# Regrouping the weight loads of a one-core decode step: larger rows, 128 partitions for wo, earlier issue

## The chip, the cores and the metric

One core of a Trainium2 chip runs the whole kernel. The metric is the device time of one execution in microseconds. The profiler's span of the same execution is about 2 us shorter (577.9 against 579.73 in the profiled run of the kernel before). Each run carries a state: slow when it lies more than 1.5% above the fastest run of the same kernel, else fast. The times come from several chips of the same kind, so kernels are compared where possible on one chip, together with runs of the kernel before.

In the views, PE is the matrix engine (TensorE) and PEld its weight loads, DVE is VectorE, ACT is ScalarE, POOL is GpSimd, and SP is the engine that issues the loads (SPq: its waits). A packet is one row that one DMA engine moves (the 256 K and V tiles of 128 rows are 32768 packets of 6144 bytes). The chain of waits is the work that ended last, followed backwards, at each step to what released it; its shares are shares of the span. The granted clock is PE's clock in the profile as a share of full speed (mean 0.976 in the profiled run of the kernel before). Partitions are the rows of a tile in on-chip memory: the K and V tiles have 128, wo_b has 64.

## The reference

A decode step for 4 sequences with a hidden size of 640: layer norm, then sliding-window attention over a K/V cache (32 heads of 192, a window of 2048 positions) and a SwiGLU feed-forward block in parallel, both added to the input.

```python
xn = layernorm(x)                                # [4, 1, 640], bf16 inputs
q = (xn @ wq).reshape(B, Sq, 32, 192)            # wq [640, 6144]
k = k_cache[:, :, Sk - 2048:, :]                 # [4, 32, 2048, 192], v the same
p = softmax(q @ k.T * 192 ** -0.5)
attn = (p @ v).reshape(B, Sq, 6144) @ wo         # wo [6144, 640]
ffn = (silu(xn @ w1) * (xn @ w3)) @ w2           # F = 1536
return x + attn + ffn
```

K and V are 201 of the 223 MB that are read. The weights are the other 22 MB.

## The kernel before

The work is cut into 128 units (32 heads by 4 sequences). Per unit DVE multiplies the K tile with the broadcast q, PE sums the products over the head dimension with identity matmuls (the "adder"), DVE reduces, ACT takes exponentials, and PE multiplies with the V tile (o_ps, here "p@v"). Eight units (two heads) make a group. There are 16 groups, and each needs 384 columns of wq and 384 rows of wo. The program is written in slots. A scheduler turns it into one fixed instruction order per engine at compile time. All loads are issued by one engine (SP) into one queue, in order; 16 DMA engines work on it. The code is shortened; a comment that starts with "..." says what was left out.

```python
def load_k(u):                                   # V alike: 128 partitions, rows of 6144 bytes
    kt = kpool.tile([P, NJ, Dh], BF16, tag="kt")
    nc.sync.dma_start(out=kt[:], in_=k_win[b, h].rearrange("(p j) d -> p j d", p=P))

def wq_load(hg):                                 # rows of 768 bytes
    wt = wpool.tile([P, KC, QW], BF16, tag="w")
    nc.sync.dma_start(out=wt[:], in_=A_wq[:, hg * QW:(hg + 1) * QW].rearrange("(kc p) n -> p kc n", p=P))

def wo_load(hg):                                 # rows of 1280 bytes; DA = 128, Dh - DA = 64
    wo_rows = A_wo[hg * QW:(hg + 1) * QW, :].rearrange("(h d) n -> d h n", d=Dh)
    wo_a = wopool.tile([DA, HG, D], BF16, tag="wo_a")
    nc.sync.dma_start(out=wo_a[:], in_=wo_rows[0:DA])
    wo_b = wopool.tile([DB, HG, D], BF16, tag="wo_b")       # 64 partitions
    nc.sync.dma_start(out=wo_b[:], in_=wo_rows[DA:Dh])

def ge_tot(hg):                                  # per group: row sums of the softmax, on PE
    tb = ps_t.tile([P, G], FP32, tag="t")
    nc.tensor.matmul(tb[:], lhsT=ones_ff[:], rhs=rsums.pop(hg)[:], start=True, stop=True)
    o_raw = ...                                  # ... cut: copy of o_ps, then ge_tr transposes it (gp),
                                                 # ge_copy normalises it, ge_proj multiplies with wo (acc)
# ... cut: the w1 and w3 chunks are loaded inside the slot that uses them (rows of 1024 bytes),
# ... cut: w2 is loaded in three parts behind everything else (rows of 1280 bytes)
```

## Time and profile before

| | before |
|---|---|
| time, median of 4 runs | 580.06 us (579.49 to 581.16) |
| mean load rate over the span | 386 GB/s |
| PE, DVE, ACT busy | 84%, 57%, 18% |
| share of DMA in the chain of waits | 74% |

The first fence has lines of the profile page of the kernel before: busy time by engine, the load rate in 40 equal slices of the span, the load queue (packets, MB, share), and the chain of waits by engine.

```profile
PE 488.1 (84%) x2391; PEld 204.7 (35%) x2391; DVE 330.1 (57%) x385; ACT 106.7 (18%) x407; POOL 3.5 (1%) x18
...
GB/s 308 416 406 417 405 378 407 395 371 403 369 408 409 376 412 370 417 402 384 406 376 416 373 409 407 370 410 365 418 385 394 407 374 414 367 418 400 390 370 136
...
q1 hardware_dynamic: 59552, 222.98, 100.2%
...
DMA 74%; PE 15%; DVE 8%; ACT 1%; SPq 1%; issue 1%; DVEq 0%; ACTq 0%
```

The queue is busy for the whole span (100.2% of 16 engines) and the chain of work that ended last is mostly loads. The kernel is bound by its loads. The slices show that the rate is not even: between the second slice and the last but one it swings between 365 and 418 GB/s.

The windows view of the same run shows where. Its columns are the stretch in us, then its length, the busy time and count for PE, weight loads, DVE, ACT and POOL, then the granted clock, the DMA share and GB/s.

```profile
60.00:65.00 5.00, 3.34 (x16) 1.40 (x17) 3.15 (x5) 0.18 (x1) 0.00 (x0) 1.00 1.02 417
190.00:195.00 5.00, 5.00 (x27) 2.01 (x26) 3.01 (x4) 0.96 (x2) 0.00 (x0) 1.00 1.04 302
225.00:230.00 5.00, 4.99 (x26) 2.06 (x25) 3.09 (x5) 0.96 (x2) 0.00 (x0) 1.00 1.05 304
```

From 60 to 65 us only K and V tiles are loaded: 417 GB/s. At 190 and at 225 us a wo load passes: 302 and 304 GB/s, although the DMA engines are as "busy" as elsewhere (1.04 and 1.05). Busy DMA engines are not fast DMA engines.

### The profile page before, as it was taken

The numbers are of one execution on the slowest core, as the hardware profiler recorded it, in microseconds if no ns is written. First come the engines' busy times: TensorE is split into PE (matmuls) and PEld (weight loads), VectorE is DVE, ScalarE is ACT, GpSimd is POOL, SyncE is SP. The second block draws the span as 40 slices with busy tenths as digits, with TensorE's granted clock in tenths as the row PEclk, the third lists the DMA queues.
The fourth block names the chain that finished last, engine by engine and source line by source line (L and its number), as shares of the span: only waits on it lengthen the run. The fifth ranks groups of instructions, "written<-read, shape, count | busy, mean of one in ns | idle before, by whom it ended". The sixth has DMA issues, their size and how long they took to land.

```text
span 577.9 us, 6288 instructions
## 1 busy us (share of the span) xinstructions
PE 488.1 (84%) x2391; PEld 204.7 (35%) x2391; DVE 330.1 (57%) x385; ACT 106.7 (18%) x407; POOL 3.5 (1%) x18
## 2 busy tenths in 40 slices
PE   2989889799798889797798988889897888978796
PEld 0334333233334334333343433334333333433343
DVE  4976645536555565565646565565555656656511
ACT  4122121312242202121021211102121120211110
POOL 2000000000000000000000000000000000000000
PEclk9999998969999999999998989999899999999999
DMA  8999999999999999999999999999999999999993
GB/s 308 416 406 417 405 378 407 395 371 403 369 408 409 376 412 370 417 402 384 406 376 416 373 409 407 370 410 365 418 385 394 407 374 414 367 418 400 390 370 136
DMA packets 59581, 223.37 MB, mean 386 GB/s; under 512 B 5016, under 2 KB 26784, under 8 KB 59552
## 3 DMA queue, kind: packets, MB, share of 16 engines
q1 hardware_dynamic: 59552, 222.98, 100.2%
q8 instruction: 18, 0.29, 0.2%
q14 instruction: 11, 0.09, 0.0%
HBM read 222.96 MB, written 0.01 MB: 386 GB/s over the span
## 4 chain that ended last, share of the span: by engine, by line
DMA 74%; PE 15%; DVE 8%; ACT 1%; SPq 1%; issue 1%; DVEq 0%; ACTq 0%
DMA kt<-in_A_k_cache_dram 52%; DMA vt<-in_A_v_cache_dram 12%; DVE pr L193 6%; PE ps L207 6%; DMA wt<-in_A_wq_dram 5%; PE o_ps L264 4%; DMA w3t<-in_B_w_dram 2%; DMA wo_b<-in_A_wo_dram 2%; DVE sc L216 1%; PE qp L177 1%; SPq L105 1%; PE bp L186 1%; PE acc L311 1%; PE f L419 0%; PE ut L340 0%
## 5 line engine op out<-in xcount | busy, mean ns | idle before, releaser
L193 DVE TENSOR_TENSOR pr<-kt,qbc 128x3072 bf16<-128x3072 bf16 x128 | 224.5, 1756 | 146.4 <-DMA kt<-in_A_k_cache_dram 142.9
L264 PE MATMUL o_ps<-vt,z 128*16 128x384 bf16 x1024 | 203.2, 330 | 45.9 <-DMA vt<-in_A_v_cache_dram 41.9
L207 PE MATMUL ps<-pr,idb 128*128 128x512 bf16 x768 | 199.2, 393 | 23.4 <-DVE sc L216 22.3
L207 PEld LDWEIGHTS <-idb 128*128 128x128 bf16 x768 | 70.4, 99 | 160.9 <-issue 106.4
L264 PEld LDWEIGHTS <-z 128*16 128x16 bf16 x1024 | 82.5, 90 | 119.8 <-issue 59.9
L216 DVE TENSOR_REDUCE sc<-ps 128x16 f32<-128x512 f32 x128 | 87.2, 682 | 0.9 <-PE ps L207 0.9
L242 ACT ACTIVATE negm<-mt 128x4 f32<-128x4 f32 x32 | 5.5, 173 | 254.9 <-PE mt L239 254.9
L187 ACT CAST qbc<-bp 128x384 bf16<-128x384 f32 x64 | 28.9, 478 | 50.2 <-PE bp L186 50.2
L250 ACT ACTIVATE z<-sc,negm 128x16 bf16<-128x16 f32 x128 | 37.8, 297 | 1.1
L272 ACT COPY o_raw<-o_ps 16x384 f32<-16x384 f32 x16 | 7.5, 467 | 106.2 <-PE o_ps L264 106.2
L233 DVE TENSOR_REDUCE gmax<-mt 4x1 f32<-4x128 f32 x32 | 8.8, 275 | 31.2 <-PE mt L228 31.2
L250 ACT ACTIVATION_READ_ACCUMULATOR z<-sc,negm 128x1 f32 x128 | 23.9, 187 | 0.0
L295 DVE TENSOR_TENSOR oT<-gp,rtb 128x8 bf16<-128x8 f32 x16 | 2.7, 167 | 30.9 <-PE gp L288 30.9
L186 PE MATMUL bp<-qsb,idb 4*128 4x384 bf16 x64 | 19.3, 341 | 1.1 <-ACT qsb L179 0.9
L177 PE MATMUL qp<-wt,xnT 128*4 128x384 bf16 x80 | 17.2, 349 | 0.3 <-DVE xnT L166 0.3
L278 DVE RECIPROCAL rtb<-tb 128x8 f32<-128x8 f32 x16 | 3.3, 207 | 24.4 <-PE tb L270 24.4
L239 PEld LDWEIGHTS mt<-idf,gmax 4*128 4x128 f32 x64 | 9.3, 182 | 10.1 <-issue 8.9
L239 PE MATMUL mt<-idf,gmax 4*128 4x4 f32 x64 | 12.1, 258 | 0.4 <-DVE gmax L233 0.4
L311 PE MATMUL acc<-wo_a,oT 128*4 128x512 bf16 x32 | 12.4, 388 | 0.0
L311 PE MATMUL acc<-wo_b,oT 64*4 64x512 bf16 x32 | 12.2, 381 | 0.0
L186 PEld LDWEIGHTS <-idb 4*128 4x128 bf16 x64 | 5.0, 93 | 17.9 <-issue 13.7
L311 PEld LDWEIGHTS <-oT 128*4 128x4 bf16 x64 | 5.1, 80 | 13.7 <-issue 11.8
(67 smaller groups left out, 151.3 us busy)
## 6 DMA issues: line engine op xcount, KB each, us to landing
kt<-in_A_k_cache_dram SPq DMA_DIRECT2D x128, 768.0 KB, 14.1
vt<-in_A_v_cache_dram SPq DMA_DIRECT2D x128, 768.0 KB, 14.0
wt<-in_A_wq_dram SPq DMA_DIRECT2D x16, 480.0 KB, 14.6
wo_a<-in_A_wo_dram SPq DMA_DIRECT2D x16, 320.0 KB, 14.2
wo_b<-in_A_wo_dram SPq DMA_DIRECT2D x16, 160.0 KB, 13.7
w1t<-in_B_w_dram SPq DMA_DIRECT2D x3, 640.0 KB, 13.9
w3t<-in_B_w_dram SPq DMA_DIRECT2D x3, 640.0 KB, 14.7
w2t<-in_B_w_dram SPq DMA_DIRECT2D x3, 640.0 KB, 11.9
```

What stands on the lines that cost most here:

```text
L177: nc.tensor.matmul(qp[:], lhsT=xnT[:, kc, :], rhs=wt[:, kc, :], start=(kc == 0), stop=(kc == KC - 1))
L186: nc.tensor.matmul(bp[:], lhsT=idb[0:B, b:b + 1].to_broadcast([B, P]), rhs=qsbs[hg][:], start=True, stop=True)
L187: nc.scalar.copy(out=qbcs[hg][:, b, :], in_=bp[:])
L193: mi = nc.vector.tensor_tensor(out=pr[:], in0=kts.pop(u)[:], in1=qbcs[hg][:, b, hl * Dh:(hl + 1) * Dh].unsqueeze(1).to_broadcast([P, NJ, Dh]),
L207: nc.tensor.matmul(ps[:, e], lhsT=idb[:], rhs=pr[:, :, kk * DD:(kk + 1) * DD], start=(kk == 0), stop=(kk == NK - 1))
L216: ri = nc.vector.tensor_reduce(out=scs[t][:, off:off + UPT, :], in_=pss.pop(m)[:], axis=AX.X, op=ALU.add)
L233: nc.vector.tensor_reduce(out=gmax[:], in_=chs[t][1][0:SB, 0:P], axis=AX.X, op=ALU.max)
L239: nc.tensor.matmul(mt[:, P:P + SB], lhsT=gmax[:, 0:1].to_broadcast([SB, P]), rhs=idf[0:SB, 0:SB], start=True, stop=True)
L250: nc.scalar.activation(out=zs[u % NZ][:, :, 2 * (G - 1):2 * G], in_=sc[:, b, :].rearrange("p (jj two) -> p jj two", two=2), func=ACTF.Exp, ...
L264: nc.tensor.matmul(o_ps[:], lhsT=z[:, jj, 2 * (G - 1 - g):2 * (2 * G - 1 - g)], rhs=vt[:, 2 * jj:2 * jj + 2, :], start=(g == 0 and jj == 0 ...
L272: nc.scalar.copy(out=o_raw[:], in_=o_pss.pop(hg)[:])
L311: nc.tensor.matmul(acc0[:], lhsT=lt, rhs=wo_t[:, hl, 0:N0], start=st, stop=sp)
```

## The change

The intent: fewer and larger packets for all weights, and weights there before they are needed. The diff is shortened, and its lines in plain words sum up what stands there.

```diff
-    def wq_load(hg):
-        wt = wpool.tile([P, KC, QW], BF16, tag="w")
+    def wq_load(ci):                       # first group alone, then 4 groups per load: rows of 3072 bytes
+        wt = wpool.tile([P, KC, cn * QW], BF16, tag="w")
...
     def wo_load(hg):
-        wo_a = wopool.tile([DA, HG, D], BF16, tag="wo_a")
-        nc.sync.dma_start(out=wo_a[:], in_=wo_rows[0:DA])
-        wo_b = wopool.tile([DB, HG, D], BF16, tag="wo_b")
-        nc.sync.dma_start(out=wo_b[:], in_=wo_rows[DA:Dh])
+        wo_t = wopool.tile([NPW, RW * D], BF16, tag="wo")          # NPW = 128, RW = 3: rows of 3840 bytes
+        nc.sync.dma_start(out=wo_t[:], in_=A_wo[hg * QW:(hg + 1) * QW, :].rearrange("(p r) n -> p (r n)", r=RW))
...
     def ge_tr(hg):                         # o_raw now bf16; output rows dealt out so that wo's rows are contiguous
-        4 fp32 matmuls into gp
+        for i in range(RW):
+            for h in range(HG):            # 12 small bf16 matmuls
+                nc.tensor.matmul(gp[h * PH:(h + 1) * PH, i, :], lhsT=o_raw[:, i:Dh:RW], ...)
     def ge_proj(hg, hl):
-        8 matmuls with wo_a and wo_b per group
+        6 matmuls with wo_t per group
...
-            add(uf - G - 2, 0, wq_load, hg)
+            if wq_chunks[ci][0] == hg:
+                add(max(uf - 2 * G, -KPF), 0, wq_load, ci)         # issued earlier
+    add(fs - 4, 0, ffn_load, "w1")         # w1 and w3 whole: rows of 3072 bytes, ahead of their use
+    add(fs - 2, 0, ffn_load, "w3")
...
-    w2 in three loads, rows of 1280 bytes
+    w2t = wpool.tile([P, FC, D], BF16, tag="w")                    # one load, rows of 15360 bytes
+    nc.sync.dma_start(out=w2t[:], in_=B_w2.rearrange("(p c) n -> p c n", c=FC))
```

More of the change, by code (lines that the diff above doesn't have):

```diff
@@ L41 @@
     RLAG: int = 2,
+    WBUFS: int = 3,
+    WQG: int = 4,
 ):
@@ L70 @@
     N1 = D - N0
+    DH2 = Dh // 2
+    assert Dh % 2 == 0 and DH2 <= P
     KPF = KBUFS - 1
@@ L74 @@
     const = ctx.enter_context(tc.tile_pool(name="const", bufs=1))
-    wpool = ctx.enter_context(tc.tile_pool(name="wstream", bufs=3))
+    wpool = ctx.enter_context(tc.tile_pool(name="wstream", bufs=WBUFS))
     kpool = ctx.enter_context(tc.tile_pool(name="kt", bufs=KBUFS))
@@ L106, in load_v @@
         vts[u] = vt
-    def wq_load(hg):
-        wt = wpool.tile([P, KC, QW], BF16, tag="w")
-        nc.sync.dma_start(out=wt[:], in_=A_wq[:, hg * QW:(hg + 1) * QW].rearrange("(kc p) n -> p kc n", p=P))
-        wqts[hg] = wt
-    def wo_load(hg):
-        wo_rows = A_wo[hg * QW:(hg + 1) * QW, :].rearrange("(h d) n -> d h n", d=Dh)
-        wo_a = wopool.tile([DA, HG, D], BF16, tag="wo_a")
-        nc.sync.dma_start(out=wo_a[:], in_=wo_rows[0:DA])
-        wo_b = None
-        if DB > 0:
-            wo_b = wopool.tile([DB, HG, D], BF16, tag="wo_b")
-            nc.sync.dma_start(out=wo_b[:], in_=wo_rows[DA:Dh])
-        wos[hg] = (wo_a, wo_b)
+    wq_chunks = [(0, 1)]
+    g0 = 1
+    while g0 < NG:
+        wq_chunks.append((g0, min(WQG, NG - g0)))
+        g0 += WQG
+    wq_of_group = {}
+    for ci, (cg0, cn) in enumerate(wq_chunks):
+        for gg in range(cg0, cg0 + cn):
+            wq_of_group[gg] = ci
+    def wq_load(ci):
+        cg0, cn = wq_chunks[ci]
+        wt = wpool.tile([P, KC, cn * QW], BF16, tag="w")
+        nc.sync.dma_start(out=wt[:], in_=A_wq[:, cg0 * QW:(cg0 + cn) * QW].rearrange("(kc p) n -> p kc n", p=P))
+        wqts[ci] = wt
+    RW = 3
+    PH = Dh // RW
+    NPW = HG * PH
+    def wo_load(hg):
+        wo_t = wopool.tile([NPW, RW * D], BF16, tag="wo")
+        nc.sync.dma_start(out=wo_t[:], in_=A_wo[hg * QW:(hg + 1) * QW, :].rearrange("(p r) n -> p (r n)", r=RW))
+        wos[hg] = wo_t
     x_sb = const.tile([B, D], BF16, name="x_sb")
@@ L173, in q_proj @@
     def q_proj(hg):
-        wt = wqts.pop(hg)
+        ci = wq_of_group[hg]
+        wt = wqts[ci]
+        c0 = (hg - wq_chunks[ci][0]) * QW
         qp = ps_t.tile([B, QW], FP32, tag="t")
         for kc in range(KC):
-            nc.tensor.matmul(qp[:], lhsT=xnT[:, kc, :], rhs=wt[:, kc, :], start=(kc == 0), stop=(kc == KC - 1))
+            nc.tensor.matmul(qp[:], lhsT=xnT[:, kc, :], rhs=wt[:, kc, c0:c0 + QW], start=(kc == 0), stop=(kc == KC - 1))
+        if hg == wq_chunks[ci][0] + wq_chunks[ci][1] - 1:
+            wqts.pop(ci)
         qsb = small.tile([B, QW], BF16, tag="qsb", bufs=2)
@@ L270, in ge_tot @@
         nc.tensor.matmul(tb[:], lhsT=ones_ff[:], rhs=rsums.pop(hg)[:], start=True, stop=True)
-        o_raw = small.tile([2 * G, 2 * Dh], FP32, tag="o_raw", bufs=2)
+        o_raw = small.tile([2 * G, 2 * Dh], BF16, tag="o_raw", bufs=2)
         nc.scalar.copy(out=o_raw[:], in_=o_pss.pop(hg)[:])
@@ L282, in ge_tr @@
         rtb, o_raw = ges[hg]
-        gp = ps_t.tile([P, 2 * G], FP32, tag="t")
-        nc.tensor.matmul(gp[0:DA, 0:G], lhsT=o_raw[:, 0:DA], rhs=idf[0:2 * G, 0:2 * G:2], start=True, stop=False)
-        nc.tensor.matmul(gp[0:DA, 0:G], lhsT=o_raw[:, Dh:Dh + DA], rhs=idf[0:2 * G, 1:2 * G:2], start=False, stop=True)
-        if DB > 0:
-            nc.tensor.matmul(gp[0:DB, G:2 * G], lhsT=o_raw[:, DA:Dh], rhs=idf[0:2 * G, 0:2 * G:2], start=True, stop=False)
-            nc.tensor.matmul(gp[0:DB, G:2 * G], lhsT=o_raw[:, Dh + DA:2 * Dh], rhs=idf[0:2 * G, 1:2 * G:2],
-                             start=False, stop=True)
+        gp = ps_t.tile([P, RW, G], FP32, tag="t")
+        for i in range(RW):
+            for h in range(HG):
+                nc.tensor.matmul(gp[h * PH:(h + 1) * PH, i, :], lhsT=o_raw[:, i:Dh:RW], rhs=idb[0:2 * G, 0:2 * G:2],
+                                 start=True, stop=False)
+                nc.tensor.matmul(gp[h * PH:(h + 1) * PH, i, :], lhsT=o_raw[:, Dh + i:2 * Dh:RW],
+                                 rhs=idb[0:2 * G, 1:2 * G:2], start=False, stop=True)
         ges[hg] = [rtb, gp]
@@ L293, in ge_copy @@
         rtb, gp = ges[hg]
-        oT = small.tile([P, 2 * G], BF16, tag="oT", bufs=2)
-        nc.vector.tensor_tensor(out=oT[0:DA, 0:G], in0=gp[0:DA, 0:G], in1=rtb[0:DA, :], op=ALU.mult)
-        if DB > 0:
-            nc.vector.tensor_tensor(out=oT[0:DB, G:2 * G], in0=gp[0:DB, G:2 * G], in1=rtb[0:DB, :], op=ALU.mult)
+        oT = small.tile([P, RW, B], BF16, tag="oT", bufs=2)
+        for h in range(HG):
+            ps = slice(h * PH, (h + 1) * PH)
+            cs = slice(h * B, (h + 1) * B)
+            nc.vector.tensor_tensor(out=oT[ps], in0=gp[ps, :, cs],
+                                    in1=rtb[ps, cs].unsqueeze(1).to_broadcast([PH, RW, B]), op=ALU.mult)
         ges[hg] = [oT]
@@ L301, in ge_proj @@
         oT = ges[hg][0]
-        wo_a, wo_b = wos[hg]
-        first = (hg == 0 and hl == 0)
-        last = (hg == NG - 1 and hl == HG - 1)
-        parts = [(oT[0:DA, hl * B:(hl + 1) * B], wo_a)]
-        if DB > 0:
-            parts.append((oT[0:DB, G + hl * B:G + (hl + 1) * B], wo_b))
-        for pi, (lt, wo_t) in enumerate(parts):
-            st = first and pi == 0
-            sp = last and pi == len(parts) - 1
-            nc.tensor.matmul(acc0[:], lhsT=lt, rhs=wo_t[:, hl, 0:N0], start=st, stop=sp)
+        wo_t = wos[hg]
+        n = RW // HG + (RW % HG if hl == HG - 1 else 0)
+        i0 = hl * (RW // HG)
+        for i in range(i0, i0 + n):
+            st = hg == 0 and i == 0
+            sp = hg == NG - 1 and i == RW - 1
+            lt = oT[0:NPW, i, :]
+            nc.tensor.matmul(acc0[:], lhsT=lt, rhs=wo_t[:, i * D:i * D + N0], start=st, stop=sp)
             if N1 > 0:
-                nc.tensor.matmul(acc1[:], lhsT=lt, rhs=wo_t[:, hl, N0:D], start=st, stop=sp)
+                nc.tensor.matmul(acc1[:], lhsT=lt, rhs=wo_t[:, i * D + N0:(i + 1) * D], start=st, stop=sp)
         if hl == HG - 1:
@@ L321, with ffn_load @@
     ffn_state = {}
+    def ffn_load(which):
+        wt = wpool.tile([P, KC, F], BF16, tag="w")
+        src = B_w1 if which == "w1" else B_w3
+        nc.sync.dma_start(out=wt[:], in_=src.rearrange("(kc p) n -> p kc n", p=P))
+        ffn_state[which] = wt
     def ffn_gate(nch):
-        w1t = wpool.tile([P, KC, NCH], BF16, tag="w")
-        nc.sync.dma_start(out=w1t[:], in_=B_w1[:, nch * NCH:(nch + 1) * NCH].rearrange("(kc p) n -> p kc n", p=P))
+        w1t = ffn_state["w1"]
         gt = ps_t.tile([B, NCH], FP32, tag="t")
         for kc in range(KC):
-            nc.tensor.matmul(gt[:], lhsT=xnT[:, kc, :], rhs=w1t[:, kc, :], start=(kc == 0), stop=(kc == KC - 1))
+            nc.tensor.matmul(gt[:], lhsT=xnT[:, kc, :], rhs=w1t[:, kc, nch * NCH:(nch + 1) * NCH],
+                             start=(kc == 0), stop=(kc == KC - 1))
         g_bf = small.tile([B, NCH], BF16, tag="g_bf", bufs=2)
@@ L333, in ffn_gate @@
         ffn_state[nch] = sg
+        if nch == F // NCH - 1:
+            ffn_state.pop("w1")
     def ffn_up(nch):
-        w3t = wpool.tile([P, KC, NCH], BF16, tag="w")
-        nc.sync.dma_start(out=w3t[:], in_=B_w3[:, nch * NCH:(nch + 1) * NCH].rearrange("(kc p) n -> p kc n", p=P))
+        w3t = ffn_state["w3"]
         ut = ps_t.tile([B, NCH], FP32, tag="t")
         for kc in range(KC):
-            nc.tensor.matmul(ut[:], lhsT=xnT[:, kc, :], rhs=w3t[:, kc, :], start=(kc == 0), stop=(kc == KC - 1))
+            nc.tensor.matmul(ut[:], lhsT=xnT[:, kc, :], rhs=w3t[:, kc, nch * NCH:(nch + 1) * NCH],
+                             start=(kc == 0), stop=(kc == KC - 1))
         u_bf = small.tile([B, NCH], BF16, tag="u_bf", bufs=2)
@@ L343, in ffn_up @@
         ffn_state[("u", nch)] = u_bf
+        if nch == F // NCH - 1:
+            ffn_state.pop("w3")
     def ffn_h(nch):
@@ L351, in ffn_transpose @@
         for fc in range(FC):
-            nc.tensor.transpose(out=hT_ps[:, fc, :], in_=h_sb[:, fc * P:(fc + 1) * P], identity=idb[0:B, 0:B])
+            nc.tensor.transpose(out=hT_ps[:, fc, :], in_=h_sb[:, fc:F:FC], identity=idb[0:B, 0:B])
         ffn_state["hT_ps"] = hT_ps
@@ L380 @@
         if hg >= 1:
-            add(uf - G - 2, 0, wq_load, hg)
+            ci = wq_of_group[hg]
+            if wq_chunks[ci][0] == hg:
+                add(max(uf - 2 * G, -KPF), 0, wq_load, ci)
             add(uf - G + 1, 6, q_proj, hg)
@@ L412 @@
         f1 = ps_m.tile([B, N1], FP32, tag="mt")
-    W2C = 4
-    for c0 in range(0, FC, W2C):
-        w2t = wpool.tile([P, W2C, D], BF16, tag="w")
-        nc.sync.dma_start(out=w2t[:], in_=B_w2[c0 * P:(c0 + W2C) * P, :].rearrange("(c p) n -> p c n", p=P))
-        for c in range(W2C):
-            fc = c0 + c
-            nc.tensor.matmul(f0[:], lhsT=hT[:, fc, :], rhs=w2t[:, c, 0:N0], start=(fc == 0), stop=(fc == FC - 1))
-            if N1 > 0:
-                nc.tensor.matmul(f1[:], lhsT=hT[:, fc, :], rhs=w2t[:, c, N0:D], start=(fc == 0), stop=(fc == FC - 1))
+    w2t = wpool.tile([P, FC, D], BF16, tag="w")
+    nc.sync.dma_start(out=w2t[:], in_=B_w2.rearrange("(p c) n -> p c n", c=FC))
+    for fc in range(FC):
+        nc.tensor.matmul(f0[:], lhsT=hT[:, fc, :], rhs=w2t[:, fc, 0:N0], start=(fc == 0), stop=(fc == FC - 1))
+        if N1 > 0:
+            nc.tensor.matmul(f1[:], lhsT=hT[:, fc, :], rhs=w2t[:, fc, N0:D], start=(fc == 0), stop=(fc == FC - 1))
     ffn_bf = const.tile([B, D], BF16, name="ffn_bf")
```

## The prediction

> **What bounds the kernel.** The HBM loads. The page gives one load queue with packets taking 100.2% of 16 engines' span, 223 MB at a mean of 386 GB/s; PE is busy 84%, DVE 57%; the chain of waits is 74% DMA. But 386 is an average of two regimes. In a window that holds only K and V loads (60 to 65 us, windows view) the rate is 417 GB/s; where a weight load passes it drops: 304 GB/s at 225 to 230 us and 302 at 190 to 195 us (both a wo load), about 392 near wq and w1/w3 loads. The packet records of the trace say why: a 6144-byte K/V packet takes 238 ns in clean stretches, a 768-byte packet (wq) about 39 ns, 1024 (w1, w3) 53, 1280 (wo, w2) 69: roughly 0.038 ns per byte plus 7 to 9 ns.
>
> The wo windows are worse than small packets explain: while wo_b (64 partitions) lands, K/V packets themselves stretch to 300-480 ns and wo packets from 55 to about 100. The wo_a part before it (128 partitions, the same 1280 bytes) runs at 55 ns with K/V at 238. So the main loss is the 64-partition load. [...]
>
> **What the change does to that.**
> - wo: one 128-partition load of 3840-byte rows instead of 128 + 64 partitions of 1280. From 225 to 235 us the mean is 360 GB/s against 417: 1.4 us lost per group, 16 groups, 22 us. I expect 1-2 us left: saves about 20 us.
> - wq: 768 to 3072 bytes (15 groups in 4 loads): loses about 0.3 us per group now, saves 3.5 us.
> - w1/w3: 1024 to 3072 bytes: saves 1.5 us. They also come early instead of in the slot that uses them.
> - w2: one load of 15360-byte rows: its data moves about 1 us faster, but the 24 final matmuls (12 pairs of 0.28 us) now all wait for the whole tile, so about +2 us in the tail.
> - Compute: 4 fp32 transposing matmuls per group (two passes each, 1.3 us) become 12 small bf16 ones; 8 acc matmuls become 6. Neutral within 0.5 us per group, off the critical path.
>
> As the queue is the bound, all of its saving is on the critical path until PE binds. PE's 488 us of work would be 88-89% busy. Check by packet sum: now 581 us per engine; at 239 ns per K/V packet and the line above for the larger packets, 548 (estimate). So 547 by that sum, 555 by the windows with the longer tail.
>
> **Predicted: 552 us, 8 in 10 between 543 and 563.** Faster by over 2%: 0.95; within 2%: 0.045; slower: 0.005.
>
> **What would show it.** Mean rate about 405 GB/s; no 5-us window near 300 in the middle; wo windows above 390; K/V packets averaging under 242 ns; DMA packets falling from 59.5 to about 41 thousand, with under 1000 below 2 KB apart from semaphore writes; PE about 88% busy; after the last V tile a tail of 11-13 us.
>
> **What would make it wrong.** (1) PE paces: its lumps of work fill the buffers and the queue waits for PE, so time stays near 560. (2) A 1.9 MB weight load, 4.7 us of queue, or the second wq chunk that waits for PE to free its buffer, stalls the K/V stream and the queue runs dry. (3) The wo slowdown comes from its place in the stream, not from the 64 partitions, and stays. (4) The w2 load as one tile lengthens the tail more than 2 us.

## More of the kernel before

What SP, the issuer, waits for most (the first two lines of the waits view; us in total, times, longest us):

```profile
SPq L99 <- DMA kt<-in_A_k_cache_dram: 85.4, 52, 3.0
SPq L105 <- DMA vt<-in_A_v_cache_dram: 81.4, 54, 2.5
```

It waits for older loads to land, which fits a full queue. Two of PE's waits are needed later:

```profile
PE o_ps L264 <- DMA vt<-in_A_v_cache_dram: 41.9, 51, 2.0
...
PE tb L270 <- ACT z L250: 1.6, 1, 1.6
```

PE waits 41.9 us for V tiles, and 1.6 us, once, between the exponentials and the row-sum matmul tb.

## The result

The changed kernel takes 556.0 us (median of 11 runs: three slow ones at 561.33 to 561.9, the fast ones at 552.46 to 556.2) against 580.02 us (16 runs). The ratio is 0.9571, with a 95% interval of 0.9555 to 0.9588. Such ratios are the mean time of one kernel's fast runs over that of the other's in the same rounds, so they are not quite the ratio of the medians. The lines below come from control a_again (555.93 us, ratio 0.9575).

The page of the changed kernel, the same lines as before:

```profile
PE 484.8 (87%) x2423; PEld 198.9 (36%) x2423; DVE 326.3 (59%) x385; ACT 106.6 (19%) x405; POOL 3.5 (1%) x18
...
GB/s 325 419 418 416 418 409 412 417 411 417 416 414 418 416 417 414 416 415 413 417 416 417 417 417 417 415 419 408 417 415 417 418 416 416 415 405 416 380 308 151
...
q1 hardware_dynamic: 43920, 222.98, 98.8%
...
PE 71%; DMA 12%; DVE 8%; ACT 7%; issue 1%; ACTq 0%
```

The rate is now even, 405 GB/s or more from the second slice to the thirty-seventh, and the queue's packets fell from 59552 to 43920. But the chain of waits has changed sides: 71% PE, where it was 74% DMA. In the 38th and 39th slice the rate falls to 380 and 308 GB/s, where the kernel before had 390 and 370.

Windows of the same run: K and V only, then two with a wo load.

```profile
60.00:65.00 5.00, 5.00 (x27) 2.24 (x27) 3.46 (x4) 0.17 (x1) 0.00 (x0) 1.00 1.02 420
185.00:190.00 5.00, 3.43 (x19) 1.70 (x19) 2.59 (x4) 1.44 (x9) 0.00 (x0) 1.00 1.02 418
215.00:220.00 5.00, 3.43 (x19) 1.62 (x17) 2.38 (x4) 1.45 (x9) 0.00 (x0) 1.00 1.02 415
```

The wo windows are at 418 and 415 GB/s where they were at 302 and 304. Two of PE's waits, and the first line of the issuer's:

```profile
PE tb L288 <- ACT z L268: 20.4, 13, 1.6
...
PE o_ps L282 <- DMA vt<-in_A_v_cache_dram: 4.1, 3, 2.3
```

```profile
SPq L109 <- PE o_ps L282: 75.1, 30, 5.9
```

PE hardly waits for V tiles any more (4.1 us, was 41.9), and the issuer's longest wait in total is now for PE to free a V buffer (75.1 us, was 34.2). tb's wait went from 1.6 to 20.4 us: 13 times in 16 groups PE, whose instructions stand in one compiled order, is idle for 1.6 us.

The packet records of the traces give the queue's work by packet size. This table is computed from them: packets, mean ns of one, and the sum over all packets divided by 16 engines. Its last row also has the 4-byte semaphore writes (3.0 and 2.5 us) and two small queues of instruction loads; the 125.6 ns are the mean of all 3072-byte packets together.

```
                       before                       changed (a_again)
K, V      6144 B   32768 x 246.8 = 505.5 us     32768 x 239.5 = 490.5 us
wq         768 B   10240 x  38.8 =  24.8          640 x  38.5 =   1.5
wq   3072, 2304 B                                1920 x 125.6 and 640 x 98.8 = 19.0
w1,w3     1024 B    3840 x  53.0 =  12.7         1280 x 125.6 (3072 B) = 10.1
wo, w2    1280 B    7688 x  68.8 =  33.1
wo        3840 B                                 2048 x 152.2 =  19.5
w2       15360 B                                  128 x 581.6 =   4.7
all                             580.7 us                        549.5 us
```

From the medians of the kernel before (36 ns for 768 bytes, 239 for 6144) a line has 0.038 ns per byte and 7 ns per packet, an estimate.

The queue lost 31 us of work. Half of it, 15 us, is in the K and V packets, which the change doesn't touch.

### The profile page after: what moved, and what is told of

Read it like the earlier page. It is cut to its first block, busy times and chain, and to the rows that moved or that the text cites. A ratio compares the mean times of both kernels' runs of the same rounds, so it can differ in the third digit from the quotient of the medians.

```text
span 559.6 us, 6310 instructions
## 1 busy us (share of the span) xinstructions
PE 487.7 (87%) x2423; PEld 200.1 (36%) x2423; DVE 325.4 (58%) x385; ACT 106.6 (19%) x405; POOL 3.5 (1%) x18
## 2 busy tenths in 40 slices
DMA packets 43950, 223.38 MB, mean 399 GB/s; under 512 B 4488, under 2 KB 5136, under 8 KB 43792
## 3 DMA queue, kind: packets, MB, share of 16 engines
q1 hardware_dynamic: 43920, 222.98, 98.3%
## 4 chain that ended last, share of the span: by engine, by line
PE 74%; DMA 9%; ACT 7%; DVE 7%; issue 1%; ACTq 0%
PE ps L225 31%; PE o_ps L282 29%; DVE pr L211 5%; DMA wt<-in_B_w_dram 4%; ACT z L268 3%; DMA kt<-in_A_k_cache_dram 3%; PE qp L193 3%; PE bp L204 3%; DMA vt<-in_A_v_cache_dram 3%; PE acc L329 2%; DVE sc L234 1%; ACT qbc L205 1%; ACT o_raw L290 1%; PE tb L288 1%; PE mt L257 1%
## 5 line engine op out<-in xcount | busy, mean ns | idle before, releaser
L225 PE MATMUL ps<-pr,idb 128*128 128x512 bf16 x768 | 209.1, 414 | 9.9 <-DVE sc L234 8.9
L282 PE MATMUL o_ps<-vt,z 128*16 128x384 bf16 x1024 | 210.1, 340 | 5.2 <-DMA vt<-in_A_v_cache_dram 3.3
L282 PEld LDWEIGHTS <-z 128*16 128x16 bf16 x1024 | 84.8, 92 | 132.8 <-issue 80.7
L316 DVE TENSOR_TENSOR oT<-gp,rtb 64x12 bf16<-64x12 f32 x32 | 5.4, 168 | 39.6 <-PE gp L306 39.1
L288 PE MATMUL tb<-rsum,ones_ff 128*128 128x8 f32 x32 | 6.6, 279 | 20.4 <-ACT z L268 20.4
L290 ACT CAST o_raw<-o_ps 16x384 bf16<-16x384 f32 x16 | 7.5, 467 | 80.3 <-PE o_ps L282 80.3
L193 PE MATMUL qp<-wt,xnT 128*4 128x384 bf16 x80 | 19.3, 358 | 0.7 <-DVE rtb L296 0.3
L197 ACT CAST qsb<-qp 4x384 bf16<-4x384 f32 x16 | 7.4, 464 | 61.0 <-PE qp L193 61.0
L329 PE MATMUL acc<-wo_t,oT 128*4 128x512 bf16 x48 | 16.7, 389 | 0.6 <-DVE oT L316 0.4
L304 PE MATMUL gp<-idb,o_raw 16*64 16x8 bf16 x96 | 6.3, 188 | 8.4 <-ACT o_raw L290 8.4
## 6 DMA issues: line engine op xcount, KB each, us to landing
wt<-in_B_w_dram SPq DMA_DIRECT2D x2, 1920.0 KB, 20.4
```

What stands on the lines that cost most here:

```text
L193: nc.tensor.matmul(qp[:], lhsT=xnT[:, kc, :], rhs=wt[:, kc, c0:c0 + QW], start=(kc == 0), stop=(kc == KC - 1))
L225: nc.tensor.matmul(ps[:, e], lhsT=idb[:], rhs=pr[:, :, kk * DD:(kk + 1) * DD], start=(kk == 0), stop=(kk == NK - 1))
L282: nc.tensor.matmul(o_ps[:], lhsT=z[:, jj, 2 * (G - 1 - g):2 * (2 * G - 1 - g)], rhs=vt[:, 2 * jj:2 * jj + 2, :], start=(g == 0 and jj == 0 ...
L290: nc.scalar.copy(out=o_raw[:], in_=o_pss.pop(hg)[:])
L329: nc.tensor.matmul(acc0[:], lhsT=lt, rhs=wo_t[:, i * D:i * D + N0], start=st, stop=sp)
```

## The experiments

Theory: before, the queue is the bound, and the largest loss is the 64-partition load wo_b, through what it does to the packets beside it. After, PE takes over in part, so not all of the queue's gain is seen. Rivals: small packets as such are the loss; and, for what is left, the queue is still the bound.

### a_again: the control

No edit.

> The changed kernel once more, for a profile in the fast state; a control. Expected by every theory: 552 to 557 us, DMA packets 43950, K/V packets at a mean of 240 to 241 ns. Theory 'PE took over as the bound': the chain of waits is mostly PE here too (over 50%), and the DMA rate has holes in the second half. Rival 'the queue is still the bound, only faster': the chain is mostly DMA in the fast state and the PE chain belongs to the slow state alone.

It ran in 555.93 us (4 fast runs), with K/V packets at 239.5 ns and a chain of 71% PE.

### wo_only: the kernel before with the wo part alone

```diff
# kernel before, with wo_load, ge_tot, ge_tr, ge_copy and ge_proj of the changed kernel; nothing else
```

> The kernel before with only the wo part of the change (one load of 128 partitions and 3840-byte rows, the new transposing and output matmuls). Theory 'wo_b was the main loss': about 20 of the 24 us gained, so 558 to 563 us; windows with a wo load at over 390 GB/s. Rival 'the small packets of wq, w1 and w3 matter as much': at least 568 us.

It ran in 557.09 us (557.03 to 557.17), ratio 0.9593, a little faster than the expected 558 to 563. On the same chip that is 23.3 of the 24.5 us of the whole change. Two windows, the first with all 128 packets of a wo load, the second just behind it, and the chain by engine:

```profile
185.00:190.00 5.00, 5.00 (x28) 2.19 (x27) 3.88 (x5) 0.96 (x2) 0.00 (x0) 1.00 1.01 412
190.00:195.00 5.00, 3.83 (x22) 1.69 (x19) 2.89 (x5) 1.18 (x8) 0.00 (x0) 1.00 1.02 418
```

```profile
DMA 80%; PE 10%; DVE 7%; issue 1%; ACT 1%; SPq 1%; ACTq 0%; DVEq 0%
```

With the wo load the rate is 412 GB/s, behind it 418, and this kernel is bound by the queue: its chain is 80% DMA. By the packet records the queue's work fell from 580.7 to 556.7 us, 15.2 us of it in K/V packets (246.8 to 239.4 ns). The part also takes work from PE (busy 465.5 us, was 488.1), but b_light below shows that less PE work brought the kernel before nothing.

### all_but_wo: the rest without the wo part

```diff
# changed kernel, with wo_load and the ge_ functions of the kernel before
```

> The changed kernel with the wo part put back as before (two loads, of 128 and of 64 partitions). Theory 'wo_b was the main loss': 570 to 577 us, wo windows near 300 GB/s as before. Rival 'small packets of wq, w1, w3': 562 us or less.

It ran in 575.36 us, ratio 0.9914: the rest alone is worth 5 us. A window with a wo load:

```profile
190.00:195.00 5.00, 3.43 (x19) 1.61 (x19) 2.82 (x4) 1.45 (x9) 0.00 (x0) 1.00 1.05 311
```

311 GB/s: the slow windows are back with wo_b. Alone the two parts bring 23.3 and 5.1 us, together 24.5. So 3.9 us of the sum were missing: the rest added 1.2 us to the wo part. On another chip it added more; see wo_early.

### wo1280: 128 partitions, but the old packet size

```diff
-        nc.sync.dma_start(out=wo_t[:], in_=A_wo[...].rearrange("(p r) n -> p (r n)", r=RW))
+        wo_rows = A_wo[hg * QW:(hg + 1) * QW, :].rearrange("(p r) n -> p r n", r=RW)
+        for i in range(RW):
+            nc.sync.dma_start(out=wo_t[:, i * D:(i + 1) * D], in_=wo_rows[:, i, :])
```

> The changed kernel with each wo group loaded by three loads of 128 partitions with 1280-byte rows into the same tile: the packet size of before, the partitions of after. Theory '64 partitions are what hurts': within 3 us of the changed kernel (552 to 559), 1280-byte packets at 55 to 60 ns, K/V packets beside them at 238 to 242 ns, wo windows over 395 GB/s. Rival 'the packet size of 1280 bytes hurts': wo windows near 300 GB/s and 570 us or more.

It ran in 558.45 us (553.75 to 560.16), ratio 0.9604 with an interval of 0.9552 to 0.9657. Two windows with a wo load:

```profile
185.00:190.00 5.00, 3.43 (x19) 1.62 (x18) 2.38 (x4) 1.45 (x9) 0.00 (x0) 1.00 1.03 404
215.00:220.00 5.00, 3.43 (x19) 1.59 (x18) 2.55 (x3) 1.45 (x9) 0.00 (x0) 1.00 1.03 400
```

404 and 400 GB/s, 1280-byte packets at 57.3 ns and K/V packets at 239.8 ns. In the kernel before, the same packet size gave 302 GB/s, 68.8 and 246.8 ns. The packet size is not what slowed the wo windows; it costs 2.5 us of queue work in wo's own packets (22.0 against 19.5). Nor is it wo's place in the stream or the number of its loads: the place is the same, and here there are three loads per group.

### wo64: 64 partitions, but larger packets

```diff
-    RW = 3
+    RW = 6        # 64 partitions, rows of 7680 bytes; transposes and output matmuls follow from it
```

> The changed kernel with the wo tile on 64 partitions with 7680-byte rows (one load, larger packets than in the change). Theory '64 partitions are what hurts, whatever the packet size': wo windows near 300 GB/s or lower, K/V packets beside it at 280 to 400 ns, 575 to 595 us (all of wo, not a third of it, now goes to 64 partitions). Rival 'packet size': wo windows over 395 GB/s, and within 6 us of the changed kernel, which would be PE's added small matmuls.

It ran in 617.58 us, ratio 1.0633, slower than the kernel before and slower than I expected. Two windows with a wo load:

```profile
160.00:165.00 5.00, 3.43 (x20) 1.57 (x19) 1.22 (x4) 1.45 (x9) 0.00 (x0) 1.00 1.06 223
195.00:200.00 5.00, 3.43 (x20) 1.75 (x20) 2.25 (x4) 1.45 (x9) 0.00 (x0) 1.00 1.05 221
```

223 and 221 GB/s with the largest packets that wo had in any run. One 7680-byte packet took 577 ns, as long as a 15360-byte packet of w2 on 128 partitions (586 ns in the same run): half the rate. Why 64 partitions get half, the runs do not show. The neighbours paid too: K/V packets rose to a mean of 254.2 ns; against the 239.5 of a_again that is 30 us of queue work on packets that didn't change, and wo's own packets added only 17 (19.5 to 36.9). The other weights' packets added about 6. The span grew by 61 us; the remaining 7 us are time in which the queue moved nothing, and whether the 288 added PE matmuls made it so is not tested. So the 64 partitions are the cause of the slow wo windows, and wo1280 and wo64 together rule the packet size out as the main one.

### b_light and a_light: less work for PE

```diff
-        for kk in range(NK):          # 6 adder matmuls per unit
+        for kk in range(NK // 2):     # 3: the result is wrong on purpose
```

> The kernel before with the same 3 of 6 adder matmuls left out (wrong on purpose). Theory 'the kernel before is bound by the queue': 577 to 581 us, no change. Rival 'PE was already a bound before': 573 us or less.

The kernel before took 579.08 us with half of its adder matmuls gone, ratio 0.9983 (0.994 to 1.0025). PE was no bound before.

> The changed kernel with 3 of the 6 adder matmuls per unit left out (result wrong on purpose; loads, vector work and the order of the rest as they are). Theory 'PE took over': 546 to 551 us, since the queue then is the bound; its per-engine packet sum (about 549.5 us) against 556.7 in the run with only the wo part says 7 us under that run's 557. Rival 'the queue is the bound': 554 to 557.

The changed kernel took 551.76 us with the same cut, just above the range, ratio 0.9498. This was another chip than a_again's, so the step from 555.9 is an indication and not a measurement on one chip. Its rate no longer falls at the end (416 and 422 GB/s in the 38th and 39th slice), and its chain by engine is:

```profile
DMA 58%; PE 26%; DVE 9%; ACT 5%; issue 2%; SPq 0%; ACTq 0%
```

It gives the level at which the changed loads bind: about 552 us.

### ord_tb and ord_tb_r5: tb kept behind the last p@v

```diff
# shortened: the dictionary, the helper and its guard are left out
             pv_insts[u] = nc.tensor.matmul(o_ps[:], ...)
...
-        nc.tensor.matmul(tb[:], lhsT=ones_ff[:], rhs=rsums.pop(hg)[:], start=True, stop=True)
+        ti = nc.tensor.matmul(tb[:], lhsT=ones_ff[:], rhs=rsums.pop(hg)[:], start=True, stop=True)
+        tc.add_manual_dep(ti.ins, pv_insts[hg * G + G - 1].ins.name, ORDER_DEP, reason="...")   # order only
```

> The changed kernel with one issue-order edge per group: the small matmul that sums the softmax rows (tb) may not be placed ahead of the group's last p@v matmul on PE. In the changed kernel it waits 1.6 us for the exponentials in each group, 20.4 us in all, with PE in order behind it. Theory 'PE took over, and this placing is a part of it': 549 to 552 us, that wait gone, the chain mostly DMA again, PE clock higher than 0.94. Rival 'the queue is the bound of the changed kernel and PE's waits are in its slack': 554 to 557 us as before.

It ran in 552.39 us (551.21 to 553.93), ratio 0.9516, the result correct. tb's wait is gone. The time lies just above the range of the theory (549 to 552) and below that of the rival (554 to 557), and the chain is 48% DMA and 40% PE, not mostly DMA as I had expected. For a comparison on one chip it ran again, beside the changed kernel.

> The changed kernel again, on the same chip and in the same rounds as the next three, so that they can be compared with it: 554 to 557 us by every theory.

> The changed kernel with the one issue-order edge per group, again: 551 to 553.5 us if the first measurement was no luck; its interval should now lie below that of the changed kernel. If it lies within 1 us of it, the theory that PE's order cost time in the changed kernel is left without support.

On this chip the changed kernel's four fast runs were at 551.21 to 555.42 us (mean 552.85, under the 554 to 557 that I had expected by every theory; two more, 561 and 565 us, were slow), ratio 0.9529 (0.9499 to 0.9559). ord_tb had five runs at 551.13 to 554.08 (mean 552.37), ratio 0.9521 (0.9497 to 0.9544). The difference is 0.5 us and not clear of noise: the theory that tb's place costs time gets no support from the times. The profiles do differ, but that of the changed kernel is from another chip (a_again, span 554.3 us), since the one taken on this chip was slow. Its late windows (columns as before), then those of ord_tb_r5 (span 550.4 us), then the chain by engine of ord_tb_r5:

```profile
520.00:525.00 5.00, 5.00 (x28) 2.09 (x26) 2.71 (x5) 0.00 (x0) 0.00 (x0) 1.00 0.98 360
525.00:530.00 5.00, 4.33 (x22) 1.95 (x23) 3.97 (x5) 1.45 (x9) 0.00 (x0) 1.00 0.74 246
535.00:540.00 5.00, 4.86 (x38) 2.78 (x37) 0.54 (x3) 1.45 (x9) 0.00 (x0) 1.00 0.87 289
```

```profile
525.00:530.00 5.00, 4.89 (x39) 2.66 (x37) 1.20 (x5) 0.47 (x1) 0.00 (x0) 1.00 1.01 409
535.00:540.00 5.00, 4.09 (x24) 2.03 (x23) 0.00 (x0) 0.00 (x0) 0.00 (x0) 1.00 0.93 394
```

```profile
DMA 70%; PE 21%; DVE 5%; ACT 3%; issue 1%; SPq 0%; ACTq 0%
```

In the changed kernel the queue runs dry late (360, 246 and 289 GB/s) behind a PE that is busy for 4.3 to 5.0 of 5 us; with tb behind p@v the rate stays at 409 and 394, and DMA is again 70% of the chain. The issuer's wait for PE to free V buffers is 9.6 us there, against 75.1. My reading is that the changed kernel stands where two bounds meet, near 552 us for the queue and at 552 to 556 us for PE. The times do not show it: on one chip, taking tb's waits away was worth nothing clear of noise.

### wo_early: the same wait in a kernel that the queue binds

Compiled orders compared without a run show that issuing wq early is enough to move tb ahead of p@v.

```diff
# wo_only, and
-            add(uf - G - 2, 0, wq_load, hg)
+            add(max(uf - 2 * G, -KPF), 0, wq_load, hg)
```

> The run with only the wo part, with each wq load issued 6 slots earlier and nothing else: the same packets, but in the compiled PE order the tb matmul then moves ahead of the p@v matmuls in 11 of 16 groups, as in the changed kernel (found by comparing compiled orders). Theory 'early weights moved tb, and its wait costs PE time': the wait for the exponentials at 12 to 18 us where the run with only the wo part has 1.6, and 558 to 561 us. Rival 'tb's place is harmless': 557 as before, in spite of the wait.

It ran in 557.0 us (555.6 to 557.07), ratio 0.9595, as wo_only did on another chip (0.9593). The tb wait of wo_only, then the tb wait and the chain by engine of wo_early:

```profile
PE tb L269 <- ACT z L249: 1.6, 1, 1.6
```

```profile
PE tb L269 <- ACT z L249: 17.3, 11, 1.6
```

```profile
PE 46%; DMA 41%; DVE 7%; ACT 5%; issue 1%; SPq 0%; ACTq 0%; DVEq 0%
```

The wait came as forecast, the time didn't: the rival was right. With the queue as the bound (busy for 100.0% of the span), 17 us of standing PE cost nothing. PE's busy time rose too, from 465.5 to 480.2 us for the same 2423 matmuls, at a granted clock of 0.957 in place of 0.994. And the chain went from 80% DMA to 46% PE while the time stayed: a chain that turns to PE does not by itself show that PE costs time. That holds for the changed kernel's 71% as well.

This run also gives the worth of the rest of the change on this chip: from wo_early (mean 556.7 us) to the changed kernel (552.85) it is 3.8 us, and their intervals (0.9573 to 0.9616, 0.9499 to 0.9559) do not overlap. On the first chip the rest had added only 1.2 us to wo_only.

### ord_w2: w2 and its matmuls out of the tail

```diff
# ord_tb, with the w2 load, its 24 matmuls and the two copies behind them moved from the end into the slots behind ffn_hT
```

> As the run before, and the w2 load and its 24 matmuls moved from the end to the middle of the stream. If the tail behind the last load (w2, then 24 matmuls and a copy, about 7 us) counts, 549.5 to 551.5 us: the last load is then a V tile, with some 6 us of work behind it. Rival: the moved work only displaces other work and the time stays at 552.

It ran in 553.65 us (553.28 to 553.86), ratio 0.9542 (0.9519 to 0.9565). This is a miss: if anything it is slower than ord_tb on the same chip, though the intervals overlap. The end of the chain, in order of time (start us, us, what), of ord_tb_r5 and of ord_w2:

```profile
529.92 13.55 DMA w2t<-in_B_w_dram
...
546.92 0.57 ACT ffn_bf L458
...
547.68 0.48 DVE res L469
```

```profile
534.32 9.32 DMA vt<-in_A_v_cache_dram
...
543.68 1.47 PE o_ps L287 x8
...
545.18 0.48 ACT o_raw L296
...
547.54 0.68 DVE attn_bf L468
```

In both the last load lands at 543.5 to 543.6 us. Behind w2 come 24 matmuls and two small operations, and the span ends at 550.4. Behind a V tile comes a longer chain (p@v, copy, transposes, normalising, output matmuls, casts), and it ends at 551.8. The w2 load at the end was cover for that chain.

## Why the prediction was right

- **The bound before was the queue.** Right: b_light shows it.
- **wo was the largest part, about 20 us.** Right in cause and a little small: 23.3 us in wo_only. wo1280 and wo64 show that the 64 partitions did it. The prediction had read it from K/V packets stretching beside wo_b (from 238 to 300-480 ns).
- **wq 3.5 us, w1 and w3 1.5 us, w2 about 1 us.** As work of the queue this was right: 7.2 us less between wo_only (556.7) and a_again (549.5). As time it was not all there: 1.2 us on top of the wo part on one chip, 3.8 us on another (from wo_early). So the total of the first chip was in part luck: wo brought 3 us more than said and the rest 5 us less than its 6, and the 2 us of a longer tail did not come.
- **"All of its saving is on the critical path until PE binds."** Whether the condition came true is not settled. The profile of a_again speaks for the prediction's first risk ("PE paces"): a chain of 71% PE and a rate that falls at the end. But wo_early has a chain of mostly PE at no cost, and on one chip ord_tb gained nothing clear of noise. PE was put at 88-89% busy and is at 87%. Not foreseen: the new issue order, in which PE stands for 20.4 us in tb.
- **A tail longer by 2 us.** Wrong in its mechanism. From the end of the last p@v to the end of the span it took 9.8 us before and 9.1 after. In the kernel before, the 24 matmuls with w2 stood behind the last p@v as well. By the prediction's own sign, the time after the last V tile, the packet records give 11.8 us before and 13.1 after; the growth lies ahead of the end of the last p@v, which came 2.0 us after the last V packet before and 4.0 us after it now.
- **Signs.** The mean rate was 403 GB/s (about 405 said), K/V packets 239.5 ns (under 242), wo windows 418 and 415 GB/s (above 390). Packets were 43920, not 41 thousand: about 39.4 thousand carry data, and I had allowed too few for the 4488 semaphore writes.
- **Open.** What the last 0 to 4 us of the changed kernel consist of. On one chip its fast runs were at 556, on another at 552.9, and I have ord_tb beside it on the second alone. PE's clock and its order both differ between the kernels, and no run separates them: the mean granted clock of the profiled runs was 0.994 in wo_only and 0.957 in wo_early, 0.942 in a_again, 0.984 in ord_tb_r5, and 0.879 in a_light with fewer matmuls, and no run explains these figures. Of the changed kernel's 22 runs 5 were slow, and of the other kernels' runs none, ord_tb's nine among them. A version clearly faster than the changed kernel was not found.

## What to carry to other kernels

Look at the rate in windows and at the packet times of the large stream, not at how busy the DMA engines are: a small load can cost most of its price in its neighbours' packets, as the tile on 64 partitions did here (wo64 against a_again: 30 us more queue work in the K/V packets, 17 in its own). Give a load 128 partitions before you work on its packet size: here 1280-byte packets on 128 partitions took 558.45 us (wo1280), 7680-byte packets on 64 took 617.58 (wo64). When a bound is lifted by a few per cent, read the chain of waits and the rate again, because the next engine may be that near, and the compiled order of the other engines may have moved with the loads. Then test with a run on the same chip whether the new waits cost time: here taking them away gained 0.5 us, not clear of noise.
